# A transfer model, a table of shifts and the last stores, in a planned attention and MLP kernel

## The chip, the core and the metric

The kernel runs on one core of a Trainium2 chip. The metric is the device time of one execution in microseconds (us), and the median of three executions is the kernel's time. The engines are TensorE (PE), VectorE (DVE), ScalarE (ACT), GpSimd (POOL) and SyncE (SP). Each takes its own instructions strictly in the order in which they were written. PE multiplies from SBUF into PSUM; ACT and DVE read PSUM, apply the functions and write SBUF; here SP and POOL only issue transfers (DMAs).

## The reference

For 8 batches of 8 heads, 576 positions and 64 columns, a linear attention is computed: `phi(x) = [relu(x) cos, relu(x) sin]` by position, `kv = phi(k)^T v` and `z = sum phi(k)` per head, and the output `phi(q) kv / (phi(q) z + 1e-6)`. The outputs of all heads side by side give 4608 tokens of 512 columns, which go through an MLP: `h = x @ w_in` (512 to 2048), `g = relu(h)^2`, `out = g @ w_out` (2048 to 512). Inputs and the result are float32; the products here are in bfloat16 with float32 sums.

## The kernel before, in words

A batch's 576 positions are four groups of 128 (the "main" tokens, 512 in all) and a tail of 64. The eight tails together are a ninth block of 512 tokens, called block 8, which goes through the MLP last.

For a batch b the steps have these names. `ldk` and `ldq` load the main rows of k and q into one buffer, `kq`, of which there is one (1 MB each); `ldv` loads v in three parts, `ldkt` and `ldqt` the tails. `cos` and `sin` (eight for the main rows, two for the tail) turn k and q into features on ACT or DVE. `kv` is the product over positions on PE, `kvz` its copy. `qTd` transposes the q features by a DMA from SBUF to SBUF (two of 128x2048 for the main rows, numbered 0 and 1, and one for the tail, numbered 2). `num` is the product with kv, `div` the division, and `xTd` transposes the result, again by DMA. Batches 0 and 1 transpose on PE instead (`qT`, `xT`). The first MLP product is `H` for blocks 0 to 2 (plain, 8 matmuls of 256 columns a step) and `G` for blocks 3 to 8: Strassen's seven products in Winograd's form, `P1` to `P7`, 4 matmuls each, with sums `xs` of the tokens. The second product is `Y`: plain for block 0, and for the others the seven products of 16 matmuls each (1.75 us), with sums `S1` to `S4` on DVE. ACT and DVE steps that empty PSUM are `r` and `q` (relu, square) behind G, and `seed`, `u2`, `s5`, `c11`, `c12`, `c21`, `c22` behind G and Y. Stores are `st`.

The first part, up to about 17 us, is written out by hand (`begin`, L1332). Everything after it is put in order by a planner when the program is built. Each step is an `Op` (L121) with its costs by engine, the steps that it follows and its buffers. `dues` (L172) works due times back from the PE steps' times. `run` (L205) walks forward in modelled time: whenever an engine is free, it takes the ready step with the smallest key, where `o.key = o.due + SHIFT.get(o.name, 0.0)`. `SHIFT` (L23) and `PINS` (L81), which ties a step to ACT or DVE, are tables of several hundred entries. A load's or transpose's end is modelled from three numbers in its op (L760 to L905), here for a main load `(1.0, 3.4, 1.8)`, by

```
before, service, behind = o.done
dma = max(dma, free[e] + before) + service
o.end = dma + behind + CARE
```

In this model SP is free again 0.5 to 1.9 us after it takes a transfer, whatever the transfers before it are doing. `plan.given` (L1425 to L1436) states when the first loads land. The modelled times appear nowhere in the program; what remains of them is the order of the instructions on each engine and the engine of each step. On the chip every engine goes through its own list and waits wherever a semaphore tells it to.

Two limits outside the planner matter. Transfers issued by SP use eight semaphores in turn, so an issue also waits for the landing of the transfer eight issues before it. And buffers: `kq` holds one batch, so `ldk` and `ldq` of a batch wait for all main features of the batch before; `fet`, the tail's features, has one slot, so `cos` and `sin` of the next tail wait for `qTd` number 2 of the batch before. PSUM has six banks for the products (pool `x`), and each seven-product step holds a bank until ACT or DVE has read it.

The end is `plan_pair(B, True)` (L1176, called at L1488): block 8's Y with a third bank `yc`. PE's last steps there are, in order, P5, P6, P3, P7, P2, P4. `c11` copies P2's sum and `c21` P4's. `plan_store` (L1127) makes eight stores of it, of 64 rows (128 KB) each, four for `ys[0]` and then four for `ys[1]`.

Of the kernel before, what the change touches and what calls it, by code (L numbers as in the profile page):

```python
# [10 lines left out]
ALU = mybir.AluOpType  # L11
ACTF = mybir.ActivationFunctionType
F32 = mybir.dt.float32
# [8 lines left out]
CARE = 1.5  # L22
SHIFT = {  # L23
    "qT0.3": -21.9, "qT0.4": 20.1, "xT0.4": 37.6, "H0.0.00.128": 19.7, "H0.0.10.0": 36.2,
    "H0.0.01.0": 20.7, "H0.2.10.0": 17.7, "H0.3.10.0": 54.7, "H0.2.01.0": 96.3, "H0.2.01q": 28.2,
    "cos1.0": 14, "cos1.2": 14, "cos1.t": 27, "kv1": 21.7, "num1.2": 3.9, "num1.3": 18.9,
    "xT1.3": 32.2, "num1.4": -9, "xT1.4": 6.8, "Y0.7": 33.1, "Y0.14": 14.4, "ldv2.0": 17.6,
    "ldqt2.1": 89, "vs2.1": -16, "cos2.0": -27.8, "sin2.0": -14.3, "cos2.1": -20.9,
    "sin2.1": -42, "cos2.3": -7.8, "sin2.3": 17.7, "num2.0": 2.9, "num2.3": 4.6,
    "H1.0.00.0": 132.3, "H1.0.10.0": 6, "H1.0.10r": -14.5, "H1.0.01.0": 76.7, "H1.0.11.0": 7.2,  # L30
    "H1.0.11r": 6.3, "H1.1.10.0": -30.6, "H1.1.01.0": 69.5, "H1.1.11r": 16, "H1.2.10r": 7.4,
    "H1.2.11.0": 146.9, "H1.3.10.0": 31.7, "H1.3.10r": 20.4, "H1.3.01.0": 22.5, "H1.3.01q": 35.3,
    "H1.3.11r": -41.1, "H1.3.11q": -3.4, "ldv3.2": 28.1, "ldkt3.1": 7.6, "cos3.0": 11.6,
    "sin3.1": -43.1, "cos3.2": 11.2, "sin3.2": -20.8, "cos3.3": 11.8, "num3.3": -49.1,
    "div3.4": 20.2, "H2.0.00.0": 91.7, "H2.0.11.0": -9.5, "H2.1.00.0": -11.9, "H2.1.10.0": -32.5,
    "H2.1.01.0": -41.9, "H2.1.01r": 34.7, "H2.1.11.0": 16.3, "H2.2.00.0": 43.1, "H2.2.00q": 26.1,
    "H2.2.10.0": 12.9, "H2.2.01.0": 42.3, "H2.2.01r": 34.8, "H2.2.01q": 13.7, "H2.3.00.0": 14.2,
    "H2.3.10.0": 15.5, "H2.3.01.0": 62.1, "H2.3.01r": 10.8, "Y1.P3": 76.2, "Y1.P4": 40.7,
    "ldk4": -152.5, "cos4.0": 5, "cos4.1": 16.5, "sin4.2": 52.6, "cos4.3": -17.8, "sin4.t": 24,
    "kvz4": 136, "num4.1": -37, "div4.1": -17.4, "qTd4.1": 11.9, "num4.4": -32.1, "div4.4": 37.2,  # L40
    "xTd4.2": -35.8, "w1s3": 159.9, "G3.0.P5": 9, "G3.0.c11r": 13.3, "G3.0.P3": -36.3,
    "G3.0.c22r": 11, "G3.0.P4": 38.7, "G3.1.P6": -73.9, "G3.1.P3": 5.5, "G3.1.c12r": 2.8,
    "G3.1.c22q": 34.5, "G3.1.c21r": -11.3, "G3.2.P1": 16.5, "G3.2.P5": -5.5, "G3.2.P2": -40.8,
    "G3.2.P6": -35.2, "G3.2.P3": 11.6, "G3.2.c12q": 159.1, "G3.2.P7": -10.2, "G3.2.P4": -43.1,
    "G3.3.P2": -19.7, "G3.3.P6": -48.6, "G3.3.s5": -29.2, "G3.3.P3": -40.2, "G3.3.P7": -75.8,
    "G3.3.c22r": -24.2, "Y2.S4": 98.8, "Y2.P6": 39.3, "Y2.P2": 7.5, "Y2.P5": 83.5, "Y2.P3": 71.9,
    "Y2.st0": -38.1, "Y2.P4": -123.3, "ldq5": -33.5, "ldv5.0": -4.3, "ldqt5.1": -3.5,
    "vs5.0": -35.8, "vs5.1": 175.1, "cos5.0": 15.9, "cos5.1": 35.5, "cos5.2": -0.4,
    "sin5.2": 20.7, "sin5.3": 94.6, "sin5.t": 6.4, "kv5": 9.1, "kvz5": -6.6, "num5.1": -1.1,
    "div5.1": 18.1, "num5.2": 10.8, "div5.4": -85.4, "xs4.1": 35.1, "xs4.2": 78.5, "xs4.3": 84,  # L50
    "xs4.4": 41.8, "G4.0.P1": -14.2, "G4.0.seed": 13.4, "G4.0.c11r": -6.8, "G4.0.c12r": -7.8,
    "G4.0.P7": -37.8, "G4.0.P4": -45.9, "G4.0.c21r": 7.2, "G4.1.P1": -22.2, "G4.1.seed": -16.3,
    "G4.1.P5": -27.3, "G4.1.P2": -44, "G4.1.u2": 17.9, "G4.1.s5": -70.1, "G4.1.P3": -29.8,
    "G4.1.P7": -18.4, "G4.1.c22r": 6, "G4.1.c21r": 5.8, "G4.2.seed": -4.3, "G4.2.P5": 1.6,
    "G4.2.P2": 78.6, "G4.2.c11r": 4.2, "G4.2.c11q": 25.7, "G4.2.c12r": 2.4, "G4.2.c12q": 48.2,
    "G4.2.P7": -7.8, "G4.2.c21q": 15.2, "G4.3.seed": -30.4, "G4.3.P2": -103.9, "G4.3.P6": -25,
    "G4.3.s5": 24, "Y3.S2": -24.4, "Y3.S3": -8.7, "Y3.P6": 7.5, "Y3.P7": 128.3, "Y3.s5": 6,
    "Y3.c22": 5.1, "Y3.c12": 0.9, "ldq6": -14.8, "vs6.1": 101.8, "vs6.2": -15.1, "sin6.0": 53.9,
    "cos6.1": -17.1, "sin6.1": 48.4, "cos6.2": 66.5, "sin6.2": 101.4, "cos6.3": 11.8,
    "sin6.3": 3.2, "cos6.t": -24.3, "kv6": 10.3, "num6.0": 28.8, "num6.1": 22.2, "qTd6.1": -10.1,  # L60
    "div6.2": -16.3, "num6.3": -4.1, "div6.4": -59.6, "xs5.3": 63.8, "G5.0.P1": -36.9,
    "G5.0.P5": 3.8, "G5.0.c11r": -13, "G5.0.s5": 4.8, "G5.0.P3": 36.2, "G5.1.P2": 12.2,
    "G5.1.P6": 19.6, "G5.2.P1": -19.8, "G5.2.c11q": 8.1, "G5.2.P6": 14.7, "G5.2.s5": 52.8,
    "G5.2.c22r": 6, "G5.3.P5": 27.9, "G5.3.P2": 3.3, "G5.3.c11q": -4.8, "G5.3.P4": -55.4,
    "G5.3.c21r": 19.9, "Y4.S1": 32.2, "Y4.S2": 12.7, "Y4.P2": 17, "Y4.P7": 95.9, "Y4.P5": 45.1,
    "Y4.c12": -4.8, "Y4.P4": 19.9, "ldq7": -19.5, "vs7.1": -31.4, "sin7.0": 63.7, "cos7.1": 42.5,
    "sin7.2": -19.3, "cos7.3": 3.2, "kvz7": -134.2, "num7.0": -56.7, "div7.4": -13,
    "G6.0.seed": -59.2, "G6.0.P3": -32.8, "G6.1.P1": 75.4, "G6.1.c11r": 27.8, "G6.1.P6": -21.4,
    "G6.1.P3": 41.1, "G6.2.seed": -21.7, "G6.2.P5": 39.1, "G6.3.P6": -60, "G6.3.P3": 3.8,
    "G6.3.P7": -35.9, "G6.3.c22r": -20.9, "Y5.S1": 23.7, "Y5.S2": 29.9, "Y5.S3": 31.3,  # L70
    "Y5.P6": 42.6, "Y5.u2": 37.5, "Y5.P5": 55.2, "Y5.P3": 133.1, "G7.2.P1": 36, "G7.2.P3": 15.3,
    "G7.2.c12r": 16.6, "G7.2.P7": -24.8, "G7.3.P6": -17.6, "Y6.S1": 44.6, "Y6.P1": -30.1,
    "Y6.P6": 17.6, "Y6.P4": 41.9, "G8.0.seed": -7.4, "G8.1.P1": 9.8, "G8.2.P3": 28.8,
    "Y7.P6": 29.3, "Y7.P7": 38.4, "Y7.P5": 31.4, "Y8.P2": 40.9,
}
EARLY = 14
STRETCH = 1.04
EARLY_TAIL = 15
REPORT = []
PLAIN = ((1, 0), (1, 1), (2, 0), (2, 1))  # L80
PINS = {  # L81
    "ACT": (
        "vs1.0 xTc0.4 qTc1.0 qTc1.1 sin2.1 H1.0.01r H1.0.01q H1.1.11r H1.2.01q H1.2.11q vs3.1 "
        "cos3.2 H2.0.00q H2.2.11r H2.3.10r H2.3.01q vs4.1 sin4.0 kvz4 G3.1.c11q G3.2.c22q "
        "G3.3.c11q G4.0.c12q G4.1.c11q Y3.u2 Y3.s5 cos6.0 sin6.0 cos6.1 cos6.2 sin6.2 sin6.3 "
        "sin6.t G5.2.c21r G5.2.c21q G5.3.c12q G6.3.c12q G7.2.c21q"
    ),
    "DVE": (
        "xTc0.3 H0.2.00r H0.2.10q cos1.t sin1.t xTc1.1 Y0.c00 Y0.c10 vs2.0 vs2.1 cos2.1 cos2.3 "
        "sin2.3 H1.0.00q H1.0.10r H1.1.00r H1.1.01r H1.1.11q H1.2.01r H1.3.10r H1.3.01r cos3.0 "  # L90
        "cos3.3 sin3.3 cos3.t H2.0.00r H2.1.11q H2.2.00r H2.3.00r cos4.0 cos4.2 sin4.3 "
# [1436 lines left out]
```

## Time and profile before

| what | value |
|---|---|
| three executions | 287.29 us median, 286.31 to 289.38 |
| the profiled execution | 288.8 us, its span 286.3 us (2.5 us lie around the span) |
| PE busy | 269.6 us, 94% of the span |
| DVE, ACT, POOL busy | 220.2, 201.0, 29.0 us |
| mean granted PE clock | 0.986 |
| DMA | 53.00 MB, mean 185 GB/s |

The span runs from the first to the last instruction of the program, and every time below counts from its start. PE's busy time is what the profile sees between a matmul's start and its modelled end, so two matmuls in a row overlap a little, and a stop is read more exactly from the start of one matmul to the start of the next. "SPq" is SP's sequencer: its row for a transfer says how long SP was held by the issue, not how long the transfer took. The time from issue to landing is another figure.

### The profile page before, as it was taken

To read this page: it belongs to the slowest core of one execution; us is meant where nothing else is said; L and a number is where in the kernel's file an instruction comes from. 1 tells how busy PE (TensorE), PEld (TensorE's weight loads), DVE (VectorE), ACT (ScalarE), POOL (GpSimd) and SP (SyncE) were. 2 spreads that over 40 slices of the span, in tenths; PEclk is the share of its full clock that TensorE was granted. 3 is DMA by queue.
4 is the path that set the end of the run, shared out by engine and by line. 5 is a ranking of instruction groups with operands and counts; after the bars stand their busy time and mean duration, and the time that the engine had idled before them with its cause. 6 is when DMAs were issued, how large, how long until landed. Compare 5 with 4: busy or idle time off the path is not lost.

```text
span 286.3 us, 6926 instructions
## 1 busy us (share of the span) xinstructions
PE 269.6 (94%) x2835; PEld 227.5 (79%) x2835; DVE 220.2 (77%) x423; ACT 201.0 (70%) x337; POOL 29.0 (10%) x46
## 2 busy tenths in 40 slices
PE   8999999999979889899988999999999999999990
PEld 3579765888869769788876889988988888888880
DVE  1779658998964988799986997999985956966810
ACT  3769983698398596798559996977675866776510
POOL 8834661100000000000000000000000000000000
PEclk9999999999999999999997999999999999999996
DMA  6999999858999999999994799369511101101106
GB/s 235 310 207 308 319 250 338 269 145 233 342 181 221 262 299 176 294 234 261 242 269 124 185 253 303 137 165 167 36 41 76 74 2 73 76 0 76 72 3 147
DMA packets 77502, 53.00 MB, mean 185 GB/s; under 512 B 52096, under 2 KB 72576, under 8 KB 77472
## 3 DMA queue, kind: packets, MB, share of 16 engines
q1 hardware_dynamic: 70448, 38.81, 55.0%
q0 software_dynamic: 7024, 13.76, 18.4%
q8 instruction: 22, 0.36, 0.6%
q14 instruction: 8, 0.07, 0.1%
HBM read 36.70 MB, written 9.44 MB: 161 GB/s over the span
## 4 chain that ended last, share of the span: by engine, by line
PE 71%; DMA 16%; ACT 4%; SPq 2%; issue 2%; POOL 2%; DVE 1%; POOLq 0%; ACTq 0%
PE ya L535 13%; PE hps L535 12%; PE yb L535 12%; PE hb L535 10%; PE hc L535 6%; PE ha L535 6%; DMA kq<-in_q_dram 5%; PE yh L535 5%; DMA qpT<-fe 4%; DMA kq<-in_k_dram 3%; DMA qpTt<-fet 3%; PE num L535 2%; PE kz L535 2%; SPq L691 1%; ACT fe L522 1%
## 5 line engine op out<-in xcount | busy, mean ns | idle before, releaser
L535 PEld LDWEIGHTS <-w1sb 128*128 128x128 bf16 x800 | 74.1, 98 | 11.1 <-issue 2.5
L516 ACT ACTIVATE gT<-rt 128x512 bf16<-128x512 bf16 x93 | 57.8, 630 | 12.7 <-DVE rt L529 10.2
L535 PEld LDWEIGHTS <-gs 128*128 128x128 bf16 x512 | 50.4, 99 | 8.2 <-issue 1.9
L535 PEld LDWEIGHTS <-gT 128*128 128x128 bf16 x448 | 43.2, 98 | 12.5 <-ACT gT L516 1.5
L535 PE MATMUL hps<-xT,w1sb 128*128 128x256 bf16 (+1 forms) x416 | 45.4, 264 | 1.6 <-DMA xT<-xp 1.6
L522 ACT ACTIVATE fe<-kq,cols 128x1024 bf16<-128x1024 f32 (+1 forms) x35 | 35.1, 1044 | 2.5 <-DMA kq<-in_q_dram 2.0
L535 PE MATMUL ya<-w2sb,gT 128*128 128x256 bf16 x256 | 30.6, 273 | 1.7 <-ACT gT L516 1.3
L535 PEld LDWEIGHTS <-w1s 128*128 128x128 bf16 x288 | 27.6, 98 | 3.8 <-issue 0.6
L524 DVE TENSOR_SCALAR fe<-kq,cols 128x1024 bf16<-128x1024 f32 (+1 forms) x37 | 24.7, 710 | 6.3 <-DMA kq<-in_k_dram 5.4
L535 PE MATMUL hb<-xs,w1sb 128*128 128x256 bf16 x192 | 28.6, 276 | 0.9 <-ACT u L506 0.9
L518 DVE TENSOR_TENSOR gT<-rt 128x512 bf16<-128x512 bf16 x51 | 20.9, 418 | 4.5 <-ACT rt L510 4.2
L535 PE MATMUL ha<-xT,w1sb 128*128 128x256 bf16 x160 | 24.1, 273 | 0.0
L661 DVE TENSOR_TENSOR xp<-num,den 128x512 bf16<-128x512 f32 (+1 forms) x33 | 22.3, 675 | 1.1
L510 ACT ACTIVATE rt<-hps 128x512 bf16<-128x512 f32 x34 | 19.9, 591 | 3.5 <-PE hps L535 2.9
L532 DVE TENSOR_TENSOR gs<-gT 128x2048 bf16<-128x2048 bf16 x16 | 19.5, 1218 | 1.1 <-ACT gT L516 1.0
L529 DVE CUSTOM_DVE_ANT_0 rt<-hb,s 128x512 bf16<-128x512 f32 x24 | 16.4, 684 | 3.1 <-PE hb L535 2.1
L529 DVE CUSTOM_DVE_ANT_0 rt<-hc,u 128x512 bf16<-128x512 f32 x24 | 16.3, 682 | 3.2 <-PE hc L535 3.2
L535 PE MATMUL yb<-w2sb,gs 128*128 128x256 bf16 x128 | 16.3, 284 | 1.6 <-ACT yu L506 1.6
L506 ACT COPY u<-hb 128x512 f32<-128x512 f32 x23 | 13.4, 581 | 4.5 <-PE hb L535 4.5
L506 ACT COPY hb<-ha 128x512 f32<-128x512 f32 x24 | 14.0, 583 | 2.8 <-PE ha L535 1.4
L535 PE MATMUL yb<-w2t,gs 128*128 128x256 bf16 x128 | 15.3, 273 | 0.0
L535 PE MATMUL yb<-w2t,gT 128*128 128x256 bf16 x128 | 15.3, 273 | 0.0
(114 smaller groups left out, 402.4 us busy)
## 6 DMA issues: line engine op xcount, KB each, us to landing
out_dram<-y SPq DMA_DIRECT2D x16, 512.0 KB, 3.4
kq<-in_k_dram SPq DMA_DIRECT2D x6, 1024.0 KB, 6.4
vs<-in_v_dram SPq DMA_DIRECT2D x10, 512.0 KB, 5.3
kq<-in_q_dram SPq DMA_DIRECT2D x5, 1024.0 KB, 6.9
w1sb<-in_moe_w_in_dram POOLq DMA_DIRECT2D x4, 512.0 KB, 10.8
w2sb<-in_moe_w_out_dram POOLq DMA_DIRECT2D x4, 512.0 KB, 10.3
kq<-in_q_dram POOLq DMA_DIRECT2D x2, 1024.0 KB, 11.5
kq<-in_k_dram POOLq DMA_DIRECT2D x2, 1024.0 KB, 10.5
```

The lines of the kernel that those rows point to most:

```text
L506: (nc.scalar.copy if e == "ACT" else nc.vector.tensor_copy)(out=out, in_=in_)
L510: nc.scalar.activation(out=out, in_=in_, func=ACTF.Relu)
L516: nc.scalar.activation(out=out, in_=in_, func=ACTF.Square)
L518: nc.vector.tensor_tensor(out=out, in0=in_, in1=in_, op=ALU.mult)
L522: nc.scalar.activation(out=out, in_=in_, func=ACTF.Relu, scale=col)
L524: nc.vector.tensor_scalar(out=out, in0=in_, scalar1=0.0, scalar2=col, op0=ALU.max, op1=ALU.mult)
L529: nc.vector._custom_dve(dve_ops.TENSOR_ADD_SAT, out=out, in0=in0, in1=in1, s0=BIG, s1=0.0)
L532: nc.vector.tensor_tensor(out=out, in0=in0, in1=in1, op=op)
L535: nc.tensor.matmul(out=out, lhsT=lhsT, rhs=rhs, start=start, stop=stop, skip_group_check=True)
L661: nc.vector.tensor_tensor(out=x.rearrange("p (b k) (l d) -> p b k l d", b=n, l=2), in0=n4[:, :, :, 0:D].rearrange("p b (k l) d -> p b k l ...
L691: nc.sync.dma_start_transpose(out=dst, in_=src)
```

## The change

The new class `Transfers` models the queue of transfers with what each issue does to those behind it: a transpose of 2048 descriptors keeps SP until what was issued before it has nearly landed; smaller ones keep SP when more than 2500 descriptors are out; a transpose right behind loads delays them; a load behind a transpose takes 0.6 us more. Each transfer's three numbers become a latency, a service time and a count of descriptors (negative for transposes). The given landings become 0.7 to 1.7 us earlier, SP's start in the plan 46.0 us. `CARE`, `BIAS`, `EARLY`, `STRETCH` and `EARLY_TAIL` change, and the tables `SHIFT` and `PINS` are replaced whole. None of this adds or removes a load, a matmul column or a feature.

In block 8's Y, `ya` becomes two banks, one for each token tile, so `seed` becomes two copies, P2 two steps of 8 matmuls (P20, P21) and `c11` two copies. The eight last stores become four of 128 rows (256 KB). PE's last steps become P5, P6, P3, P7, P20, P21, P4. Outside block 8's Y, every step that the program had it still has, mostly at another place in its engine's order; 26 of the squares behind G and 7 of the `u2` copies behind G go from ACT to DVE.

The diff, cut to its core:

```diff
-CARE = 1.5
+CARE = 1.0
+ROOM = 2500
 SHIFT = {
-    "qT0.3": -21.9, "qT0.4": 20.1, "xT0.4": 37.6, "H0.0.00.128": 19.7, "H0.0.10.0": 36.2,
...
+    "f0.t0": 6.3, "num0.2": 2.7, "qT0.3": -27.6, "qT0.4": 1.4, "xT0.4": 31.6,
...
 }
-EARLY = 14
-STRETCH = 1.04
-EARLY_TAIL = 15
+EARLY = 20
+STRETCH = 1.08
+EARLY_TAIL = 5
 PINS = {
...
-BIAS = 0.3
+BIAS = 0
...
+class Transfers:
+    def __init__(self, at):
+        self.landed, self.turned, self.last, self.out = at, False, 0, []
+
+    def issue(self, end, lat, service, n, ring):
+        size = abs(n)
+        if ring:
+            if n < 0 and self.last >= 512 and self.landed > end - 1.0:
+                self.landed += {2048: 2.0 if self.last > 512 else 0.8, 512: 1.3}.get(size, 0.0)
+            if size >= 2048:
+                end = max(end, self.landed - 0.3)
+            else:
+                self.out = [x for x in self.out if x[0] > end]
+                while sum(x[1] for x in self.out) + size > ROOM:
+                    end = max(end, self.out.pop(0)[0])
+        if n > 0 and self.turned:
+            service += 0.6
+        self.landed = max(end + lat, self.landed + service)
+        self.turned, self.last = n < 0, n
+        if ring:
+            self.out.append((self.landed - 1.5, size))
+        return end, self.landed
...
             took = min(o.engines.values())
             if o.done is not None:
-                took += sum(o.done) + CARE
+                took += o.done[0] + CARE
...
+        transfers = Transfers(dma)
...
                 if o.done is None:
                     o.end = free[e]
                 else:
-                    before, service, behind = o.done
-                    dma = max(dma, free[e] + before) + service
-                    o.end = dma + behind + CARE
+                    free[e], landed = transfers.issue(free[e], *o.done, e == "SP")
+                    o.end = landed + CARE
@@ -768,7 +818,7 @@
-                (1.0, 3.4, 1.8),
+                (4.7, 3.1, 1024),
@@ -779,7 +829,7 @@
-                (1.0, 1.8 if i < 2 else 0.6, 1.8),
+                (3.4, 1.5, 512) if i < 2 else (2.3, 0.5, 512),
@@ -792,7 +842,7 @@
-                    (1.0, 0.3, 1.8),
+                    (2.3, 0.22, 256),
@@ -865,7 +915,7 @@
-                    (0.0, 1.5 if i < 2 else 0.3, 1.0),
+                    (2.05, 1.9, -2048) if i < 2 else (1.2, 0.55, -512),
@@ -894,7 +944,7 @@
-                    (0.0, 1.0 if i < 2 else 0.2, 1.0),
+                    (1.6, 0.95, -1024) if i < 2 else (1.1, 0.4, -256),
@@ -1119,23 +1169,22 @@
         else:
             dst = bass.AP(
                 tensor=out.tensor,
-                offset=((4 * i + 2 * t + g) * S + MAIN) * DM,
-                ap=[[DM, TAIL], [1, DM]],
-            )
-            nc.sync.dma_start(out=dst, in_=y[g * TAIL : (g + 1) * TAIL, t, :])
-
-    def plan_store(b, key, y, i, after):
-        for t, g in [(t, g) for t in range(2) for g in range(2)] if b == B else [(None, None)]:
-            o = plan.op(
-                f"{key}.st{i}{'' if g is None else (t, g)}".replace(", ", ""),
-                {"SP": 0.5},
-                lambda e, t=t, g=g: store(b, y, i, t, g),
-                after,
-                [y],
-                None,
-                (0.6, 1.35 if g is None else 0.35, 0.8),
-            )
-            o.late = 4.0
+                offset=((4 * i + 2 * t) * S + MAIN) * DM,
+                ap=[[S * DM, 2], [DM, TAIL], [1, DM]],
+            )
+            nc.sync.dma_start(out=dst, in_=y[:, t, :])
+
+    def plan_store(b, key, y, i, after, t=None):
+        o = plan.op(
+            f"{key}.st{i}{'' if t is None else t}",
+            {"SP": 0.5},
+            lambda e: store(b, y, i, t),
+            after,
+            [y],
+            None,
+            (2.3, 1.3 if t is None else 0.5, 128),
+        )
+        o.late = 4.0
@@ -1177,15 +1226,22 @@
-        acc = buf("x", [P, 2, n], F32, "ya", "full")
         run = buf("x", [P, 2, n], F32, "yb", "seed")
-        other = buf("x", [P, 2, n], F32, "yc", "full") if apart else acc
+        if apart:
+            accs = [buf("x", [P, 1, n], F32, f"ya{t}", "half") for t in range(2)]
+            other = buf("x", [P, 2, n], F32, "yc", "full")
+            A = lambda t: accs[t][:, 0]
+        else:
+            accs = [buf("x", [P, 2, n], F32, "ya", "full")]
+            other = accs[0]
+            A = lambda t: other[:, t]
...
-        def prod(m, o, lhs, rhs, first, after, space=acc):
+        def prod(m, o, lhs, rhs, first, after, spaces, t0=0, t1=2):
...
-                l_, r, a = fn(), rhs(), o()
-                for t in range(2):
+                l_, r = fn(), rhs()
+                for t in range(t0, t1):
                     for hb in range(HB2):
-                        start = first and hb == t == 0
-                        mm(a[:, t], l_[:, t, hb, :], r[:, hb, :], start, hb == HB2 - 1)
-
-            p = pe(f"{key}.P{m}", 2 * HB2 * MM, emit, after + ready, [space] + bufs)
+                        start = first and hb == 0 and (t == 0 or len(spaces) > 1)
+                        mm(o(t), l_[:, t, hb, :], r[:, hb, :], start, hb == HB2 - 1)
...
-        p1 = prod(1, A, block(0, 0), lambda: w2_block(0, 0), True, [w[0], sum5.get(b), begun.get(0)])
+            after = [w[1]] + (seeds if apart else [e11])
+            p5 = prod(5, C, summed(1), lambda: w2t[1], True, after, [other])
+            return ev("s5", flex(2), lambda e: copy(e, s5[:, :], bank(other)), [p5], [other, s5], 0.6)
+
+        after = [w[0], sum5.get(b), begun.get(0)]
+        p1 = prod(1, A, block(0, 0), lambda: w2_block(0, 0), True, after, accs)
         begun[b] = begun[0] = p1
-        seed = ev("seed", {"ACT": act(2 * n)}, lambda e: copy(e, Bb(), A()), [p1], [acc, run], 0.3)
+        seeds = [
+            ev(
+                f"seed{t or ''}",
+                {"ACT": act(2 // len(accs) * n)},
+                lambda e, t=t: copy(e, run[:, t : t + 2 // len(accs), :], bank(accs[t])),
+                [p1],
+                [accs[t], run],
+                0.3,
+            )
+            for t in range(len(accs))
+        ]
...
+        if not apart:
+            p2 = prod(2, A, block(0, 1), lambda: w2_block(1, 0), False, seeds, accs)
+            e11 = ev("c11", flex(2), lambda e: copy(e, left(0), bank(other)), [p2], accs + [ys[0]], 1.0)
...
-        plan_store(b, key, ys[0], 0, [e11, e12])
-        p4 = prod(4, Bb, block(1, 1), lambda: w2t[4], False, [e22, w[4]], run)
-        e21 = ev("c21", flex, lambda e: copy(e, left(1), Bb()), [p4], [run, ys[1]], 1.0)
-        plan_store(b, key, ys[1], 1, [e21, e22])
+        if not apart:
+            plan_store(b, key, ys[0], 0, [e11, e12])
+        p4 = prod(4, Bb, block(1, 1), lambda: w2t[4], False, [e22, w[4]], [run])
+        e21 = ev("c21", flex(2), lambda e: copy(e, left(1), bank(run)), [p4], [run, ys[1]], 1.0)
+        for t in range(2) if b == B else [None]:
+            plan_store(b, key, ys[1], 1, [e21, e22], t)
+        for t in range(2 if apart else 0):
+            p2 = prod(2, A, block(0, 1), lambda: w2_block(1, 0), False, seeds, accs[t : t + 1], t, t + 1)
+            e11 = ev(
+                f"c11{t}",
+                flex(1),
+                lambda e, t=t: copy(e, ys[0][:, t, 0:n], A(t)),
+                [p2],
+                [accs[t], ys[0]],
+                0.3,
+            )
+            plan_store(b, key, ys[0], 0, [e11, e12], t)
...
-        w1_in = [plan.given(f"w1.{i}", t) for i, t in enumerate((17.0, 19.6, 22.2, 24.8))]
-        w2_in = [plan.given(f"w2.{i}", t) for i, t in enumerate((27.8, 37.0, 42.6, 45.2))]
-        qt0 = plan.given("qt0", 25.3, [kqt[0]])
+        w1_in = [plan.given(f"w1.{i}", t) for i, t in enumerate((15.9, 18.9, 21.2, 23.7))]
+        w2_in = [plan.given(f"w2.{i}", t) for i, t in enumerate((26.6, 35.6, 41.2, 44.2))]
+        qt0 = plan.given("qt0", 24.2, [kqt[0]])
-            ("q", 31.2, kq[1]), ("k", 34.5, kq[1]),
+            ("q", 29.6, kq[1]), ("k", 32.9, kq[1]),
-        got["qt"] = [plan.given("qt1", 31.8, [kqt[1]])]
-        got["kt"] = [plan.given("kt1", 35.0, [kqt[1]])]
-        land = [plan.given(f"v1.{i}", t, [vs[1, i]]) for i, t in enumerate((38.6, 40.2, 40.5))]
+        got["qt"] = [plan.given("qt1", 30.1, [kqt[1]])]
+        got["kt"] = [plan.given("kt1", 33.3, [kqt[1]])]
+        land = [plan.given(f"v1.{i}", t, [vs[1, i]]) for i, t in enumerate((37.1, 38.5, 38.9))]
@@ -1488,7 +1577,7 @@
-        order = plan.run({"PE": 16.8, "ACT": 17.4, "DVE": 17.1, "POOL": 36.0, "SP": 1.0}, 45.0)
+        order = plan.run({"PE": 16.8, "ACT": 17.4, "DVE": 17.1, "POOL": 36.0, "SP": 46.0}, 44.2)
```

## The prediction

> **What bounds the kernel now.** I read the page's busy shares first, then a table of 8 us windows to find where PE stands still, then the chain and the timelines of PE and SP around those places.
>
> ```profile
> PE 269.6 (94%) x2835; PEld 227.5 (79%) x2835; DVE 220.2 (77%) x423; ACT 201.0 (70%) x337; POOL 29.0 (10%) x46
> PEclk9999999999999999999997999999999999999996
> 80.00:88.00 8.00, 6.44 (x88) 5.84 (x84) 4.99 (x11) 7.20 (x13) 0.00 (x0) 1.00 0.86 193
> 96.00:104.00 8.00, 6.25 (x66) 4.97 (x64) 7.24 (x13) 5.77 (x10) 0.00 (x0) 1.00 1.33 236
> 144.00:152.00 8.00, 6.03 (x67) 5.14 (x64) 7.28 (x16) 5.23 (x9) 0.00 (x0) 1.00 1.06 230
> 152.00:160.00 8.00, 8.00 (x72) 6.68 (x70) 5.30 (x12) 7.89 (x13) 0.00 (x0) 0.79 0.36 94
> 232.00:240.00 8.00, 8.00 (x76) 7.17 (x74) 4.11 (x7) 4.63 (x10) 0.00 (x0) 1.00 0.14 59
> ```
>
> The windows' columns are PE, PEld, DVE, ACT and POOL busy, granted clock, DMA. PE is the bound: from 160 us to its last matmul at 279.6 no window loses anything. What can be won lies between 64 and 160 us and behind the last matmul. Read from start to start of the matmuls on either side, the stops over 0.5 us are 0.5 (at 68.9), 0.6 (71.8), 1.7 (80.0), 1.2 (99.0), 1.4 (103.0), 1.1 (115.5), 0.6 and 1.7 (148.6 and 149.6): 8.8 us. Behind the last pair the clock is granted at 0.79 for 8 us, a loss of 0.21 x 8 = 1.7. Together 10.5.
>
> The causes stand in SP's timeline and in the chain.
>
> ```profile
> 82.20 1.78 SPq L691 DMA_TRANSPOSE qpT<-fe  x1
> 84.09 0.52 SPq L575 DMA_DIRECT2D kq<-in_k_dram  x1
> 84.71 6.32 SPq L691 DMA_TRANSPOSE qpT<-fe  x1
> 91.12 0.53 SPq L587 DMA_DIRECT2D vs<-in_v_dram  x1
> 91.70 0.50 SPq L575 DMA_DIRECT2D kq<-in_q_dram  x1
> ```
> ```profile
> 139.16 7.98 DMA kq<-in_k_dram
> 147.13 2.04 issue
> 149.80 1.13 ACT fe L522
> 150.93 0.48 ACT yu L506
> 151.45 0.60 PE yb L535 x4
> ```
>
> A main transpose that has nothing in front of it holds SP for 1.78 us; behind `ldk4` it holds SP for 6.32, to 91.03, and that load lands at 91.14. `ldq4`, free to go long before, goes out at 91.70. Behind `ldq5` the same form holds SP from 109.63 to 117.74, 8.11 us. The old model frees SP after 1.9 us in both cases. From 59.5 to 146 us SP has hardly a free moment, so each hold delays every later transfer. PE pays when ACT or DVE reaches a feature whose load is late: in the second fence ACT waits for batch 6's k, and behind its features in ACT's list stands `yu`, for which PE waits.
>
> **The order.** Main transposes directly behind a main load or one `ldv` are 2.1, 3.1, 4.1 and, with a store between, 6.1; tail ones behind main loads are 3.2, 5.2 and 6.2. In the new order 2.0 and 2.1, 3.0 and 3.1, 4.0 and 4.1 go out ahead of the next batch's main loads; left directly behind loads are 3.0 and 5.0 (behind one `ldv`), 6.0 (behind `ldk7`) and the tail 6.2. The holds over 1.78 us that go are 2.2 (3.94), 4.5 (6.32) and 6.3 (8.11): 13 us of SP before 118 us.
>
> Whether that reaches PE I follow by places: a step's place is the PE work ahead of it in the order, by the rows' durations (16 matmuls of 256 columns 1.75 us, 40 of kv 1.19, and so on), added to 18.9, where the planned part starts. `kv3` has place 84.8 before and starts at 87.0. In the new order the main features of batch 2 stand beside place 53.5 to 57.2, before 58.5 to 62.2; before they start at 57.9 though q landed at 53.05. So `kq` is free 4 to 5 us earlier, and `ldq3`, `ldk3` can go out at about 61.5 (behind two transposes) where they went at 68.07 and 68.65. The loads of batch 4 stand at 80 to 81 against 84.1 and 91.7 on the clock, those of batch 5 at 103 against 109.1 and 117.8, those of batch 6 at 131 against 138.5.
>
> What becomes late next: from a pair's issue to the landing of both took 9.98 (batch 3), 8.6 (6) and 9.86 us (7). The new distance from the later issue to the first feature is 9.1 us of PE work in batch 3, 10.6, 10.3 and 10.7 in 4 to 6, 8.3 in 7, where only q comes late and a single load took 6.46 (`ldq4`). So batch 3 is short by 0.9. `xTd2.0` waits for `ldk3`, eight issues before it, hence to 71.5; issue 1.27 and landing 3.0 in all (page median) bring it to 74.5, and its reader H2 has place 73.9: 0.6. The tail transposes 2.2, 3.2 and 4.2 now go out late, and `kv3`, `kv4`, `kv5` need the `fet` slot they free; a tail transpose landed between 1.1 and 6.5 us behind its issue's end. I cannot place these waits; their bounds are 0 and 5 us in all, and I take 2.0, two of the present eight stops at their mean of 1.1. Left: 0.9 + 0.6 + 2.0 = 3.5. The clock's 1.7 goes, because no single stop of that sum exceeds the 2.3 us lost between 148.6 and 151.4. **Middle: 10.5 - 3.5 = 7.0 saved**, between 5.5 and 10.5.
>
> On the clock the Trainium skill ("TensorE: Matmul & The Clock Gate", What's actually happening) says that the array is slowed to half after an idle window of about 3.4 us. The trace halves it for 3.41 us from 152.12, after stops of only 2.3 us, so the measurement is the stricter one. By the page alone the 1.7 would be no matter of the stops, and the saving 5.3.
>
> **ACT and DVE.** 26 squares of G move from ACT (0.63 us) to DVE (0.42), 4 of H back, 7 `u2` from 0.58 to 0.68; with the rest of the counts DVE comes to about 239 us and ACT to 177. Both stay under PE's 259 us (the 2835 matmuls at their start-to-start times, 0.109 us for 256 columns). In the windows from 160 to 264 DVE is at most 7.9 of 8 busy, so a late eviction is possible; I cost it at 0, bounds 0 and +2, because the same seven-product steps now run without a stop.
>
> **The tail.**
>
> ```profile
> 277.72 1.91 PE L535 MATMUL yb<-w2t,gT 128*128 128x256 bf16 x16
> 277.92 0.58 ACT L506 COPY y<-ya 128x512 f32<-128x512 f32 x1 [4.66 <-PE ya L535]
> 278.53 5.04 SPq L1125 DMA_DIRECT2D out_dram<-y  x8
> 279.71 0.58 ACT L506 COPY y<-yb 128x512 f32<-128x512 f32 x1 [1.21 <-PE yb L535]
> ```
> ```profile
> out_dram<-y SPq DMA_DIRECT2D x16, 512.0 KB, 3.4
> out_dram<-y SPq DMA_DIRECT2D x8, 128.0 KB, 2.4
> ```
>
> Eight issues of 0.63 us in a row hold SP from 278.53 to 283.57; the last sum is in SBUF at 280.29, so the last store goes out 2.7 us later than it could. It lands at 285.33, and the span ends at 286.3. With E for PE's end (279.63): the last full product is still P4, since P20 and P21 stand ahead of it. That the last sum is split therefore shortens nothing at the end; it lets the first two stores go out beside P4's 1.75 us. P21's copy of 128x256 has no row here; between half of 0.58 and the whole of it, it ends at most 0.8 us behind P21, and two issues of 0.63 end before P4's copy does, at E + 0.66. Then two stores: issues at E + 0.69 and E + 1.32. For 256 KB there is no row; from issue to landing a quiet 128 KB store took 2.35 us, and a quiet 512 KB one 2.59 (238.07 to 240.66), so 2.5, landing at E + 3.8. Before it was E + 5.7. **Tail: 1.9 saved**, between 1.7 and 2.0. `seed` in two copies costs ACT at most 0.58 more beside Y7's P4 (1.75). `s5` goes to DVE behind S3, 0.1 us later for P3; bounds 0 and 0.3, I take 0.
>
> **Sum.** The profiled execution took 288.8 us, 286.3 of span and 2.5 around it. 288.8 - 7.0 - 1.9 = 279.9. It was 1.5 above the median of 287.29, and the shown executions reach from 286.31 to 289.38; I forecast the median, **278.4**.
>
> **Rivals.**
> 1. *No stop left.* All 10.5 go: 287.3 - 10.5 - 1.9 = 274.9. For it: loads of batches 4 to 6 are 7 to 14 us earlier, more than any stop. Against: the two waits worked out above, 1.5.
> 2. *The order of the queue is not what PE waits for*, and the stops only change place: the tail alone, 287.3 - 1.9 = 285.4. Against it stands the fence with 6.32; for it, that DMA is over 90% busy in most slices up to 143 us, so that the bytes could be the limit whatever their order. The Trainium skill ("Advanced Engine Details and Errata", X-Bar Transpose (TRN2)) has transposing transfers as fast as ordinary ones, by which their place behind loads would not matter; the trace disagrees, 1.78 against 6.32 us for one form.
> 3. *The loads' readers stand too early.* Slower: the first features of batches 3 to 7 stand 8.3 to 10.7 us of PE work behind their loads, before 9.2 to 12. In-order ACT and DVE stop there, with evictions behind them, and a stop of 2.3 us brings half a clock for 1.7, as at batch 6: 4.0. Five such cost 20 and the removed ones give back 10.5 + 1.9: 287.3 + 7.6 = 294.9. It decides when SP's issues slip more than 2.5 us behind their places in all five, (10.5 + 1.9) / 5. Against it: the new order removes the longest holds of SP.
>
> **How the numbers follow.** Chances: forecast 0.65, rival 1 0.18, rival 2 0.10, rival 3 0.07. Under 1% is about what a measurement of this kernel cannot tell from no change. Forecast, rival 1 and 0.01 of rival 2 are faster by more (0.84); the rest of rival 2 and 0.01 of rival 3, with three waits of its five (287.3 + 12 - 12.4 = 286.9), lie within 1% (0.10); 0.06 of rival 3 is slower. The range leaves out rival 3, rival 2's upper half and the last of rival 1: from 274.5 (rival 1, with 0.4 of small stops) to 285.5 (the forecast with 5 us of unplaced stops and 2 from DVE, 283.4, and rival 2's middle).
>
> **What would show it.** Right: no main transpose of batches 2 to 4 holds SP over 3 us; `ldq3` goes out before 64 us, batch 5's pair before 107; PE's windows from 96 to 160 lose under 3 us; no granted clock under 0.9 inside; two of the last four stores behind the last copy, and the span's end about 4.8 us behind PE's end instead of 6.7. Wrong: SP held as long by other pairs, ACT or DVE waiting for k or q in more than two batches, PE windows after 160 us under 8.00, or a `kv` that waits for a tail transpose.

## The result and the profile after

The changed kernel took 302.51 us (median of four runs, 301.48 to 304.23), the kernel before 287.85 beside it: a ratio of 1.0515 [1.0436, 1.0595], slower, where 278.4 and at most 285.5 was forecast. Runs in which the chip held the clock down are left out here and below; the profiled executions of e1_eight and e3_flat were such, so of their profiles only the stretch behind PE's last matmul is read.

The page of the changed kernel (first the engines' busy times and shares, then rows of 40 slices of 7.5 us):

```profile
PE 269.3 (89%) x2831; PEld 227.2 (76%) x2835; DVE 233.4 (78%) x460; ACT 181.4 (60%) x302; POOL 28.2 (9%) x46
PE   8799999999999998999789999999999999999000
PEclk9999999999999999999979999999999999999755
DMA  7999999899999999599938994651320300110111
```

PE's busy time is what it was (269.6), but its share fell from 94 to 89%: three slices at the end are empty of PE, and the DMA row there reads 1, a tenth. The timeline of the end:

```profile
276.12 9.90 SPq L1175 DMA_DIRECT2D out_dram<-y  x4
276.26 1.91 PE L585 MATMUL yb<-w2t,gT 128*128 128x256 bf16 x16
276.46 0.37 ACT L556 COPY y<-ya 128x256 f32<-128x256 f32 x1 [0.46 <-PE ya L585]
278.21 0.58 ACT L556 COPY y<-yb 128x512 f32<-128x512 f32 x1 [1.38 <-PE yb L585]
```

PE's last matmul ends at 278.17, in the profile before at 279.63; the last copy is done at 278.79. The span ends at 300.9, **22.7 us behind PE's end**, where the profile before had 6.7. What runs in these 22.7 us stands in the windows of 8 us (columns as in the prediction: busy times, then granted clock, DMA share, GB/s):

```profile
280.00:288.00 8.00, 0.00 (x0) 0.00 (x0) 0.00 (x0) 0.00 (x0) 0.00 (x0) 0.63 0.13 49
288.00:296.00 8.00, 0.00 (x0) 0.00 (x0) 0.00 (x0) 0.00 (x0) 0.00 (x0) 0.50 0.13 51
```

and, for comparison, the same stretch of the kernel before:

```profile
280.00:288.00 8.00, 0.00 (x0) 0.00 (x0) 0.00 (x0) 0.30 (x1) 0.00 (x0) 0.61 0.54 126
```

Only the four last stores are left, 1 MB in all. A share of 0.13 can be two of sixteen DMA engines at work all the time, or sixteen at work an eighth of it; the packets' own records in the trace decide. From 281 to 300 us two packets are under way 90% of the time and three nearly all the rest, and each store's landing is marked by two engines (the first at 284.33 and 284.34). In the kernel before, from 281 to 285 us, 12 to 16 packets are under way 86% of the time, and each store's landing has sixteen marks. So two engines carry the four stores. 50 GB/s over two is 25 GB/s for each; 1 MB at 50 GB/s is 21 us. The issues themselves, free at first (0.68 and 0.53 us), then took 2.15 and 5.01 us.

In the middle, the windows that the prediction showed:

```profile
80.00:88.00 8.00, 8.00 (x109) 7.21 (x108) 7.93 (x14) 6.18 (x11) 0.00 (x0) 1.00 1.06 271
96.00:104.00 8.00, 8.00 (x84) 6.99 (x83) 7.93 (x15) 7.72 (x12) 0.00 (x0) 1.00 1.08 201
144.00:152.00 8.00, 5.26 (x58) 4.22 (x56) 5.25 (x13) 3.67 (x6) 0.00 (x0) 1.00 0.85 264
152.00:160.00 8.00, 8.00 (x65) 6.27 (x63) 6.37 (x15) 6.37 (x11) 0.00 (x0) 0.79 0.56 122
```

The losses of batches 3 and 4 are gone (6.44 and 6.25 before, 8.00 now). Batch 6's is larger (6.03 before, 5.26 now), and so the clock of 0.79 behind it is still there. PE's stops over 0.4 us from 20 us on, from start to start, are 0.44 (53.6), 0.70 (75.0), 1.27 (119.1) and 2.73 (148.5), with the clock's 1.7 together 6.8 instead of 10.5: **3.7 saved, 7.0 forecast**. SP around the loads of batches 3, 4 and 6, and the chain (start, length, what) around the two stops:

```profile
61.81 0.46 SPq L625 DMA_DIRECT2D kq<-in_q_dram  x1
62.33 0.75 SPq L625 DMA_DIRECT2D kq<-in_k_dram  x1
...
76.91 5.27 SPq L741 DMA_TRANSPOSE qpT<-fe  x2
82.24 0.58 SPq L625 DMA_DIRECT2D kq<-in_k_dram  x1
...
127.23 8.47 SPq L741 DMA_TRANSPOSE qpT<-fe  x2
...
138.41 0.50 SPq L625 DMA_DIRECT2D kq<-in_k_dram  x1
138.96 0.57 SPq L625 DMA_DIRECT2D kq<-in_q_dram  x1
```
```profile
108.90 9.37 DMA kq<-in_k_dram
119.06 0.75 DVE fe L574
...
138.96 6.33 DMA kq<-in_q_dram
145.30 4.33 issue
149.67 1.01 issue
150.68 0.59 ACT rt L560
151.31 0.60 PE hc L585 x4
```

`ldq3` goes out 6.8 us earlier than before (68.65), and PE no longer stops for the loads of batches 3 and 4; the 0.70 at 75.0 is H2's wait for `xTd2.0`. Batch 6's pair goes out at 138.41 and 138.96, where the kernel before had 138.5 and 139.2. ACT's features stand at the head of its list and start at 149.63; behind them stands `rt`, for which PE waits. The 4.33 us before that are "issue", a wait for which the chain names nothing. The trace's semaphores name it: ACT and DVE both wait there for the semaphore of `ldq6`, whose last mark comes at 149.56, 10.6 us behind its issue (fifteen of its sixteen marks are there by 147.85; why the last is late is not known). `ldk6` had landed at 144.97. What an earlier issue of the pair is worth, e4_loads6_early tests. The first two rows of the chain show batch 5's late load, with DVE in ACT's place.

### The profile page after: what moved, and what is told of

Read it like the earlier page. It is cut to its first block, busy times and chain, and to the rows that moved or that the text cites. A ratio compares the mean times of both kernels' runs of the same rounds, so it can differ in the third digit from the quotient of the medians.

```text
span 300.9 us, 6915 instructions
## 1 busy us (share of the span) xinstructions
PE 269.3 (89%) x2831; PEld 227.2 (76%) x2835; DVE 233.4 (78%) x460; ACT 181.4 (60%) x302; POOL 28.2 (9%) x46
## 4 chain that ended last, share of the span: by engine, by line
PE 57%; DMA 21%; DVE 5%; issue 4%; POOL 3%; SPq 2%; ACT 1%; POOLq 0%; DVEq 0%
PE ya L585 14%; PE yb L585 13%; PE hb L585 9%; DMA kq<-in_k_dram 7%; PE hc L585 6%; PE ha L585 6%; DMA vs<-in_v_dram 6%; PE hps L585 5%; DMA w1sb<-in_moe_w_in_dram 4%; DMA kq<-in_q_dram 2%; DMA xT<-xp 2%; PE kz L585 2%; PE num L585 2%; DVE fe L574 1%; PE yc L585 1%
## 5 line engine op out<-in xcount | busy, mean ns | idle before, releaser
L566 ACT ACTIVATE gT<-rt 128x512 bf16<-128x512 bf16 x71 | 43.3, 628 | 10.7 <-DVE rt L579 8.1
L572 ACT ACTIVATE fe<-kq,cols 128x1024 bf16<-128x1024 f32 (+1 forms) x32 | 31.8, 1034 | 12.7 <-issue 4.3
L574 DVE TENSOR_SCALAR fe<-kq,cols 128x1024 bf16<-128x1024 f32 (+1 forms) x40 | 27.3, 720 | 10.2 <-DMA kq<-in_k_dram 6.9
L568 DVE TENSOR_TENSOR gT<-rt 128x512 bf16<-128x512 bf16 x73 | 29.3, 419 | 2.7 <-ACT rt L560 2.4
L585 PE MATMUL ha<-xT,w1sb 128*128 128x256 bf16 x160 | 23.7, 273 | 0.0
L560 ACT ACTIVATE rt<-hps 128x512 bf16<-128x512 f32 x30 | 17.5, 590 | 4.4 <-PE hps L585 4.3
L585 PE MATMUL hc<-xs,w1s 128*128 128x256 bf16 x96 | 14.4, 272 | 3.7 <-ACT rt L560 2.6
L556 ACT CAST vext<-vs 128x1024 bf16<-128x1024 f32 x9 | 9.4, 1046 | 10.2 <-DVE xp L711 7.1
```

The source lines that it names most:

```text
L556: (nc.scalar.copy if e == "ACT" else nc.vector.tensor_copy)(out=out, in_=in_)
L560: nc.scalar.activation(out=out, in_=in_, func=ACTF.Relu)
L566: nc.scalar.activation(out=out, in_=in_, func=ACTF.Square)
L568: nc.vector.tensor_tensor(out=out, in0=in_, in1=in_, op=ALU.mult)
L572: nc.scalar.activation(out=out, in_=in_, func=ACTF.Relu, scale=col)
L574: nc.vector.tensor_scalar(out=out, in0=in_, scalar1=0.0, scalar2=col, op0=ALU.max, op1=ALU.mult)
```

## The experiments

Two theories explain the two misses. **A**: the new store's destination has a slowest dimension of 2 (two sequences of 64 rows), so only two DMA engines carry it. The Trainium skill ("DMA: Bandwidth & Descriptors", Why a DMA increments its semaphore by 16 and not by 1) says that a transfer is spread over the largest number up to 16 that divides the slowest dimensions of both sides; the share of 0.13 and the two packets at a time above agree. **D**: batch 6's loads (and 5's) are issued too late because main transposes stand directly behind another load on SP, and PE pays for that order. Their rivals have letters of their own in the expectations: above all F, that the many-dimensional form of the store and not the divisor is slow, and G, that an earlier load is paid back by something else.

**e1_eight.** Each of the four stores as two of 64 rows, the second at the next sequence's tail (`...` marks lines left out); all else as changed.

```diff
-                ap=[[S * DM, 2], [DM, TAIL], [1, DM]],
...
-            nc.sync.dma_start(out=dst, in_=y[:, t, :])
+                ap=[[DM, TAIL], [1, DM]],
...
+            nc.sync.dma_start(out=dst, in_=y[0:TAIL, t, :])
...
+            nc.sync.dma_start(out=dst, in_=y[TAIL:P, t, :])
```

> The changed kernel, with each of its four last stores issued as two of 64 rows (slowest dimension of the destination 64 instead of 2); every order stays as it is. Theory A (a store whose destination's slowest dimension is 2 is carried by 2 of the 16 DMA engines: the share of 0.13 and 50 GB/s in the changed kernel's last 20 us): the way from PE's last matmul to the span's end falls from 22.7 us to about 6, and the time from 302.5 to about 286. Theory B (stores of more bytes at a quiet end are slow, or the last stores wait for the order): the bytes and the order are the same, so the time stays above 298. Theory C (the new order of the planner costs the time): it stays at 302.

Measured: 285.7, ratio 0.9897 [0.9806, 0.9988], the span's end 5.8 us behind PE's. The form of the store alone was worth 17 us.

**e2_two_engines_before.** The kernel before, with nothing but the two-part store.

```diff
-                ap=[[DM, TAIL], [1, DM]],
...
-            nc.sync.dma_start(out=dst, in_=y[g * TAIL : (g + 1) * TAIL, t, :])
...
+                ap=[[S * DM, 2], [DM, TAIL], [1, DM]],
...
+            if g == 0:
+                nc.sync.dma_start(out=dst, in_=y[:, t, :])
```

> The kernel before, with nothing changed but its last stores: each pair of 64 rows is one store of 128 rows with the two-part destination, issued when the first of the pair was. Theory A: 1 MB at some 50 GB/s from 278.5 us on, 21 to 24 us, so the span ends at 300 to 303 and the time is 301 to 306. Theory C: 287, as before.

Measured: 307.59 (307.22 to 307.69), ratio 1.0649 [1.056, 1.0737], 1.6 over the expected range; its PE ends at 281.28, 1.65 later than in the profile before, with other stops, and the span 23.7 behind. Its windows:

```profile
288.00:296.00 8.00, 0.00 (x0) 0.00 (x0) 0.00 (x0) 0.00 (x0) 0.00 (x0) 0.50 0.13 51
296.00:304.00 8.00, 0.00 (x0) 0.00 (x0) 0.00 (x0) 0.00 (x0) 0.00 (x0) 0.50 0.12 47
```

Two engines at the same speed, with the old order: the loss belongs to the store alone.

**e3_flat.** The changed kernel with the four stores' 128 rows in one run; half of them go to the first rows of the following sequence, so this is the same number of bytes and issues at another place.

```diff
-                ap=[[S * DM, 2], [DM, TAIL], [1, DM]],
+                ap=[[DM, P], [1, DM]],
```

> The changed kernel with its four last stores of 128 rows, but the destination's rows in one run (slowest dimension 128): the same number of stores and bytes. It leaves out the right place of the tails: half of each store's rows go to the next batch's first rows. Theory A: all 16 engines carry it, PE's end to the span's end takes 4.8 us (two issues of 0.63 behind the last copy, landing 2.5 behind the issue), and the time is about 284.6, 1 us under the one with eight stores. Theory B (256 KB stores are slow as such): above 298.

Measured: 283.23 to 283.80, ratio 0.9819 [0.9737, 0.9901], the span's end 4.5 us behind PE's. Four stores of 256 KB are no burden in themselves, and the prediction's 4.8 us fit them. Of its 2.1 us under e1_eight the end has 1.3 (4.5 against 5.8); the rest probably belongs to the middle, since the mean clock of its runs was 0.997 and e1_eight's 0.988.

**e5_rows62.** Flat stores again, but of 62 and 2 rows each, so that the slowest dimension is even and has no divisor from 3 to 16. All rows are stored at their places.

```diff
...
+                ap=[[DM, TAIL - 2], [1, DM]],
...
+            nc.sync.dma_start(out=dst, in_=y[0 : TAIL - 2, t, :])
...
+                    ap=[[DM, 2], [1, DM]],
...
+                nc.sync.dma_start(out=dst, in_=y[(g + 1) * TAIL - 2 : (g + 1) * TAIL, t, :])
```

> The changed kernel with each of its four last stores cut into flat runs of 62 and 2 rows of one tail each (sixteen stores, the same bytes, nothing two-part in any destination). Theory A as a rule on divisors (the Trainium skill, "DMA: Bandwidth & Descriptors", How many engines (k): the largest number up to 16 that divides the slowest dimensions of both sides; 62 gives 2): as slow as the two-part form, about 20 us of transfer at 50 GB/s with a DMA share of 0.13 behind PE's end, time 300 to 306. Theory F (it is the two-part destination as a shape, with its jump between tails, that is slow): flat runs are fast, and sixteen issues of 0.6 us at most, eight of them behind the last copy, put the end 7.5 to 8.5 us behind PE's, time 287 to 290.

Measured: 301.48 (one run), the span's end 22.8 behind PE's (276.50). Its windows:

```profile
280.00:288.00 8.00, 0.00 (x0) 0.00 (x0) 0.00 (x0) 0.00 (x0) 0.00 (x0) 0.50 0.13 50
288.00:296.00 8.00, 0.00 (x0) 0.00 (x0) 0.00 (x0) 0.00 (x0) 0.00 (x0) 0.50 0.13 51
```

A flat form with 62 rows is as slow as the two-part form with 2, while 64 and 128 rows are fast. So it is the divisor, and F is out.

**e4_loads6_early.** e1_eight, and on SP batch 6's loads ahead of what held them: a few operations are moved in the finished order before anything is emitted.

```diff
+        behind(("ldv6.0",), "xTd4.0")
+        behind(("ldv6.1", "ldk6", "ldq6"), "qTd5.1")
```

> The one with eight stores, and on SP alone: ldv6.0 goes out ahead of xTd4.1 instead of directly ahead of the transposes 5.0 and 5.1, and ldv6.1, ldk6 and ldq6 go out directly behind 5.1, ahead of a store and a tail transpose. Theory D (PE's stop of 2.7 us at 148.5 and the half clock behind it, 1.7, come from ldk6 and ldq6 going out at 138.4 behind those issues): they go out by 134.5, the features no longer hold up ACT and DVE, and the time is 3 to 4.5 us under the one with eight stores. Theory E (the transfers are bound by bytes there, whatever their order): the loads land at the same time and the two are equal within 1 us.

Measured: 282.89, ratio 0.9802 [0.9728, 0.9875], 2.8 under e1_eight on the same chip, 0.2 short of the expected range. SP's timeline shows the pair 4.9 us earlier than in the changed kernel, and the windows show where it went:

```profile
126.44 6.39 SPq L741 DMA_TRANSPOSE qpT<-fe  x2
133.12 0.38 SPq L637 DMA_DIRECT2D vs<-in_v_dram  x1
133.55 0.50 SPq L625 DMA_DIRECT2D kq<-in_k_dram  x1
134.10 0.57 SPq L625 DMA_DIRECT2D kq<-in_q_dram  x1
```
```profile
144.00:152.00 8.00, 7.93 (x89) 6.56 (x87) 7.83 (x17) 6.76 (x9) 0.00 (x0) 1.00 0.72 171
152.00:160.00 8.00, 8.00 (x103) 7.12 (x102) 7.93 (x19) 7.07 (x14) 0.00 (x0) 1.00 0.60 151
```

5.26 became 7.93, the features start at 144.7 without a wait, and the clock stays at 1.00. Of the 4.9 us, 2.1 come from the transposes, which hold SP for 6.39 instead of 8.47 without the load directly ahead of them, 2.0 from what the pair overtakes, and 0.8 from an earlier start of the transposes. Behind a store, with no load directly ahead, the two still hold SP for 3.0 and 3.3 us. The longest stop left is batch 5's, 1.30 us, in the same pattern (in brackets the idle time and what ended it):

```profile
117.36 3.23 ACT L572 ACTIVATE fe<-kq,cols 128x1024 bf16<-128x1024 f32 x3 [1.65 <-DMA kq<-in_k_dram]
119.47 0.60 PE L585 MATMUL hc<-xs,w1s 128*128 128x256 bf16 x4 [1.14 <-DVE rt L579]
```

**e6_loads56_early.** The same for batch 5 as well, its pair ahead of two stores.

```diff
+        behind(("ldv5.0", "ldq5", "ldk5"), "qTd4.1")
```

> The one with loads 6 moved, and besides ldv5.0, ldq5 and ldk5 directly behind the transpose qTd4.1, ahead of two stores, xTd2.2 and ldqt6.1. Theory D (PE's stop of 1.3 us at 118 comes from DVE and ACT waiting 1.5 us for ldk5, which goes out at 107.6 behind those issues): ldk5 goes out by 104.5 and lands by 115, the stop goes, and the time is 1.0 to 1.5 us under 282.9. Theory E (bound by bytes there): ldk5 lands at 117 as now and the time stays at 282.9 within 0.5.

Measured: 285.1 (ten runs), ratio 0.9918 [0.9873, 0.9963]: worse than e4_loads6_early's 0.9802 on another chip, though the two intervals just touch. The stop at 118 us is gone, but a new one stands at 111.6:

```profile
113.73 0.59 ACT L556 COPY y<-ya 128x512 f32<-128x512 f32 x1 [2.95 <-DMA out_dram<-y]
114.37 1.80 PE L585 MATMUL ya<-w2t,gs 128*128 128x256 bf16 x15 [2.51 <-ACT y L556]
```

Y1's second store, now behind 2 MB more of loads, lands at 115.10 instead of 110.78; there are two `y` buffers, the copy waits for one of them, and PE for the copy. An advanced load is not free: here it was paid back by the store that it overtook.

**e7_two_queues.** e6_loads56_early, with two of the four stores behind the last copy issued from ACT, so that two issues stand in a row on each queue instead of four on one.

```diff
-            nc.sync.dma_start(out=dst, in_=y[TAIL:P, t, :])
+            (nc.scalar if i else nc.sync).dma_start(out=dst, in_=y[TAIL:P, t, :])
```

> The one with loads 5 and 6 moved, and of the four stores behind the last copy two go out from ACT's queue instead of SP's. If the end is set by the four issues of 0.6 us in a row (274.91 to 277.31, in the kernel with loads 6 moved), two in a row on each queue end 1.2 us earlier: the span's end comes 4.5 us behind PE's end instead of 5.7, and the time falls by 1.2 against the one with one queue. If the landing sets it (a rival: two queues share the engines and land no earlier), it stays.

Measured: ratio 0.9849 [0.9764, 0.9933], an interval that overlaps e6_loads56_early's. The profile shows 0.5 us of the expected 1.2, from PE's end to the span's end 5.25 instead of 5.78. The timeline of its end:

```profile
278.04 1.11 SPq L1175 DMA_DIRECT2D out_dram<-y  x2
278.05 1.39 ACTq L1181 DMA_DIRECT2D out_dram<-y  x2
```

The last issue now ends at 279.44; four in a row would end 1.0 us later (e10_eight_again's last four take 2.40 us, from 279.04 to 281.44).

**e8_both, e9_loads6_again, e10_eight_again.** On one chip: e1_eight and e4_loads6_early again, and e4_loads6_early with the two queues and batch 5's pair behind Y1's stores instead of ahead of them.

```diff
+        behind(("ldq5", "ldk5"), "Y1.st1")
+        behind(("ldv6.0",), "xTd4.0")
+        behind(("ldv6.1", "ldk6", "ldq6"), "qTd5.1")
```

> Loads 6 moved as before; of batch 5, only ldq5 and ldk5 move, ahead of xTd2.2 and ldqt6.1 but behind both stores of Y1, whose landing at 115 instead of 111 held up Y2's copy and PE for 2.7 us at 111.6 when the loads stood ahead of them; and of the four stores behind the last copy two go out from ACT. Theory D: ldk5 goes out by 105 and lands by 115.5, Y1's stores land by 112, neither stop (1.3 at 118, 2.7 at 111.6) is left, and the end comes 5.2 us behind PE's end: 1.5 to 2 us under the kernel with loads 6 moved alone, and 2.5 to 3.5% under the kernel before. Rival G (any load that moves ahead delays another transfer by as much, since the bytes set the time): within 0.5 us of that kernel.

> The kernel with loads 6 moved once more, beside the others on the same chip: 2% under the kernel before, as on the first chip (282.9 against 288.85).

> The changed kernel with eight stores once more, beside the others on the same chip, for the stops of its order: 285.7, which is 1.1% under the kernel before; in the profile a stop of 2 to 3 us near 148 and one of 1.3 near 119, and PE's end to the span's end 5.7 us.

Measured, beside 289.94 for the kernel before: e10_eight_again 285.75, ratio 0.9871 [0.9822, 0.992]; e9_loads6_again 283.74, 0.9815 [0.9761, 0.9869]; **e8_both 282.23 (280.77 to 283.26), 0.9751 [0.9709, 0.9793]**, which beats both kernels. It is 1.5 us under e9_loads6_again, the least that was expected. In e8_both `ldk5` goes out at 105.17 instead of the changed kernel's 108.90, Y1's second store still lands at 111.27, and neither stop is left:

```profile
112.00:120.00 8.00, 8.00 (x87) 7.22 (x86) 6.43 (x14) 6.51 (x10) 0.00 (x0) 1.00 1.14 249
144.00:152.00 8.00, 8.00 (x90) 6.82 (x89) 7.83 (x17) 6.81 (x9) 0.00 (x0) 1.00 0.71 170
```

An earlier load is thus not always paid back, and G falls as a general rule; e6_loads56_early is its one case. The three together give the order a price: 3.5 us from e10_eight_again to e8_both, of which the second queue has about 0.5 (5.8 behind PE's end against 5.3).

## Why the prediction was wrong

The change comes to +14.7 by the medians. The two profiles give: the end +16.0 (22.7 instead of 6.7), PE's end -1.5.

- **The step that failed is the tail's**: "For 256 KB there is no row; from issue to landing a quiet 128 KB store took 2.35 us, and a quiet 512 KB one 2.59", hence 2.5 and a landing at E + 3.8. The two rows are of stores whose destinations have a slowest dimension of 64 and 128; the new one has 2. The size lay between the two rows, the shape did not. In place of 4.8 us behind PE's end 22.7 were measured: 17.9 of the 24.1 by which the forecast missed. The bounds of the term, 1.7 and 2.0, were made from the same two rows, and no rival held a slower store; both neighbours seemed to agree, and so the shape went unpriced. e1_eight, e2_two_engines_before, e3_flat and e5_rows62 settle it: with a slowest dimension of 128 the same four stores end 4.5 us behind PE's end.
- **The middle was mis-sized**: 3.7 instead of 7.0, and under the range's 5.5 (with waits of 0.9 and 0.6 and up to 5 unplaced, the lower end would have been 4.0). Of the 3.5 us that were to be left, H2's wait for `xTd2.0` came as worked out (0.70 for 0.6); batch 3's 0.9 did not come, and no `kv` waited for a tail transpose. In their place stand the stops of batches 5 and 6, with the clock. The list of what is "left directly behind loads" had 3.0, 5.0 and 6.0 in it, but no price. Transposes 5.0 and 5.1 held SP for 8.47 us (127.23 to 135.70), so batch 6's pair, placed at 131, went out at 138.4, as before. Nothing of batch 6 was won, and behind the stop of 2.73 us, over the 2.3 named, the clock's 1.7 was lost again. e4_loads6_early, which moves only those loads, takes away both. (That the clock falls whenever a stop is over 2.3 us is not so, see the end.) In batch 5 a wait of 1.3 us replaced the 1.1 of before; its pair went out at 108.25, 1.25 behind the mark of 107.
- **The kernel before was misread at batch 6.** The prediction has ACT waiting for batch 6's k there. That load landed at 147.13, but ACT waited on until 149.13, for the semaphore of the tail transpose 5.2, whose last mark came at 149.10: what ACT took up next was the tail's features, `fet`, whose one slot that transpose had to free.

```profile
149.17 0.72 ACT L522 ACTIVATE fet<-kqt,cols 128x512 bf16<-128x512 f32 x1 [2.74 <-issue]
149.80 1.13 ACT L522 ACTIVATE fe<-kq,cols 128x1024 bf16<-128x1024 f32 x1
```

  That transpose had been issued at 139.84, behind both loads. The k load itself held DVE alone, for 0.58 us. In the changed kernel the wait there is for a load after all, but for `ldq6`.
- **Rival 3's mechanism was right, in one batch and a half of five.** ACT and DVE stopped at late features, evictions stood behind them, and in the profiled execution half the clock followed. The chance and the price were for five batches; one alone should have stood in the forecast, where the pair's way through SP had not been followed.
- **Rival 2 is out.** With the bytes unchanged, SP's order of batch 6's loads alone moved 2.8 us on one chip and 2.0 on another (285.75 to 283.74). Against it also stands the profile after, where 6.44 became 8.00 in the window from 80 us. (The prediction's 1.78 and 6.32 are times that SP was held; how fast a transpose moves its bytes they do not show.)
- **Right**: `ldq3` before 64 us (61.81), no loss from batches 3 and 4, the windows from 160 to 272 us full but for one of 7.94 although DVE came to 233 us (239 forecast) and ACT to 181 (177); P4 last; two issues done before the last copy (at 277.43, the copy at 278.79, E + 0.62 for the E + 0.66 forecast). **Signs that were missed** besides the clock and the end: transpose 3.0, behind one `ldv`, held SP for 3.33 us where under 3 was named, and the windows from 96 to 160 us lost 3.8 us.
- **Left over**: PE's first stop differs between executions of identical instructions (0.68 us before, 1.84 after, 1.97 in e9_loads6_again, 1.21 in e2_two_engines_before), here 1.2 against the change. 3.7 - 1.2 is 2.5, and PE's end came 1.5 earlier; the 1.0 between is not placed. With it, 17.9 + 3.3 + 1.2 + 1.0 make 23.4 of the 24.1; the rest, but for rounding, is the forecast's 1.5 between profiled execution and median, which was 0.6 this time, less 0.4 because 2.1 us instead of 2.5 lay around the span. e2_two_engines_before, whose order is that of before, has stops of 3.16 at 80.6 and 2.61 at 150.1 and none at 99: one profile's stops are a sample, and the 10.5 was one too.

The plan without the store's form would have been right in sign: e10_eight_again is 4.2 us faster than before, e1_eight 3.2.

## What to carry to other kernels

When a transfer is rewritten, look first at the slowest dimension of both sides, and only then at the size: a new row is like an old one only if both are alike. A store that is last in a kernel has nothing beside it, so its whole price is on the end. A load's issue time is to be followed through each hold ahead of it on its queue; a step that is listed as "left behind a load" needs a price at once, and a load that is moved ahead needs a look at what it overtakes.

## What the runs showed that was not expected

- Two engines carried 49 to 51 GB/s whatever the row form (e2_two_engines_before, e5_rows62, the changed kernel), 25 GB/s each. With 64 rows as slowest dimension, the same megabyte was out 5.8 us behind PE's end (e10_eight_again).
- An issue that is normally 0.55 us long took 5.01 when its queue held three earlier 256 KB stores on two engines.
- The half clock does not follow from the length of a stop alone. It came for 3.4 us behind 2.73 us in the changed kernel, 3.16 in e2_two_engines_before, 3.10 in e7_two_queues, and two stops of 0.56 and 1.73 in the kernel before; it stayed at 1.00 behind 2.61 us in that same execution of e2_two_engines_before, 2.53 in e10_eight_again and 2.67 in e6_loads56_early. Where a stop lies separates them. Within one execution, half clocks start a whole multiple of 3.413 us apart: 38 times between 152.12 and 281.83 in the kernel before, and 38, 59 and 48 times in the changed kernel, e2_two_engines_before and e7_two_queues. Cut along that grid, the stretch ahead of the half clock has PE busy for 1.44, 1.11, 0.50 and 0.83 us in these four, and the stretch with most of the stop has 1.76, 1.64 and 1.62 in the three without it. From the kernel before, the changed kernel and e6_loads56_early, in this order:

```profile
148.71:152.12 3.41, 1.44 (x13) 0.98 (x12) 3.34 (x8) 2.95 (x4) 0.00 (x0) 1.00 0.80 217
149.01:152.42 3.41, 1.11 (x11) 0.99 (x11) 2.71 (x6) 2.79 (x4) 0.00 (x0) 1.00 0.42 124
110.24:113.65 3.41, 1.62 (x21) 1.33 (x20) 1.78 (x5) 0.55 (x1) 0.00 (x0) 1.00 1.03 388
```

  The Trainium skill ("TensorE: Matmul & The Clock Gate", What's actually happening) has a free-running window of about 3.4 us over which activity is watched; the trace agrees, though no run here moved a stop against the grid on purpose. So a stop of this size costs the 1.7 us in some executions and nothing of it in others. The windows of e10_eight_again, to be held against those of the changed kernel above, show the stop without the half clock:

```profile
144.00:152.00 8.00, 5.85 (x63) 4.73 (x62) 5.44 (x14) 3.70 (x7) 0.00 (x0) 1.00 0.98 309
152.00:160.00 8.00, 7.58 (x74) 6.55 (x74) 7.75 (x17) 7.73 (x13) 0.00 (x0) 1.00 0.62 127
```

- Two stores issued from ACT took 1.39 us, from SP in the same moment 1.11 (e7_two_queues).
